# One product for the scales of all units, later weight squares, and the second batch's softmax sums in SBUF

## The chip, the cores and the metric

One core of a Trainium2 chip runs the whole program. The metric is the device time of one execution in microseconds (us). Three runs of the kernel before took 861.09, 863.54 and 863.58 us; their median is 863.54 us.

## The reference

Four batches of 576 tokens with 512 features pass through three stages.

1. Memory attention, per batch and head (8 heads of 64): `a = softmax(phi)` over 32 memory slots, `k_m = aᵀk`, `v_m = aᵀv`, then `softmax(q k_mᵀ / 8) v_m`.
2. A gated layer: `(sigmoid(x w_gate) * (x w_val)) w_out`, with 1536 hidden features.
3. A routed mixture of 8 experts: noisy logits, the two best experts of each token, `relu(x w1[e]) w2[e]` weighted by a softmax over the two.

The gated layer's weights arrive as 64-bit floats and are rounded to 32 bits on the chip. Products that need more than half precision are made of a high and a low 16-bit half of each operand.

## The kernel before

The program is written as Python generators that issue instructions for a planner. The planner lists each engine's instructions in a fixed order, chosen by priority and by data that it expects to be ready; on the chip each engine then runs its list strictly in order and waits at the head of it. `behind(d, o)` adds no wait of its own on the chip; it tells the planner that `d` stands after `o` in the order. `turns(g)` advances a generator by one `yield`, so the number of yields decides where in the program a step is issued. The attention generator runs with a priority 160 positions ahead once batch 0 is done.

**Rounding the weights** (`weights`, lines 371 to 414). There are 18 jobs: for each of six units of 256 hidden features a `wg` and a `wv` job (0 to 11), then six `wo` jobs (12 to 17). Every job has two halves of 512 KB. A half is loaded by SP's queue (line 352), and `rounded` (lines 359 to 369) makes 32-bit floats of it: ScalarE scales the low words (line 363), VectorE combines the high words (lines 367 and 368; `self.shifted` is the latest instruction of line 368), GpSimd adds the two (line 369). The loads of `wo` go into a ring of four buffers (`ws2`), so each waits for the GpSimd sum of the half that used its buffer four halves earlier.

**Scales.** When a job of the first twelve is rounded, ScalarE squares all of it into a sum (line 402). The sums of a unit go through a TensorE product with ones and three small VectorE instructions in `norm2` (lines 86 to 105), which give a power-of-two scale `s` and its inverse `iv` in tiles of that unit. `finish` (line 378) runs this two yields after the first rounding of the job after the unit. `unit_scales` (line 426) multiplies each unit's scale with each batch's scale `sv[b]`, two GpSimd instructions for every pair of batch and unit, as soon as both are known (lines 433 and 435).

**Fold and first stage.** `fold(b, u)` (line 243) scales the batch's memory values on GpSimd (line 250, needs `wss` from line 433), multiplies them into the unit's weights on TensorE (line 257) and splits the product on ScalarE and VectorE (lines 259 and 261). `stage1` (line 456) makes 24 matmuls for 192 tokens and one unit (line 468, `self.gated` is the latest of them), with tanh on ScalarE (470, `gss` from line 435), a product on VectorE (472), and the high and low half of the result on ScalarE and VectorE (473, 474). Eighteen such pieces belong to batch 0; after each of them the weights advance by three yields and, early on, the attention of batch 1 by one. The first six pieces of batch 1 follow.

**Attention of a batch** (`attention`, line 266). There are three pieces: two of 512 columns and one of 128. `scores` makes the products (lines 279 and 282) in a bank of the pool `pg`, whose four banks `stage1` and `fold` use too; VectorE takes the maximum and subtracts it (286, 290), ScalarE exponentiates (291). `normalised` sums on VectorE (line 297) into the same PSUM bank, adds 1e-9 (300) and inverts (301), and GpSimd multiplies (302). `turned` transposes on TensorE (310) and splits into `x` (317, 318). Batch 0 does its three sums after its three scores; the others do each sum right after its scores, in the same step.

**After that** come the `wo` scale and its splits (410 to 418), the second product (`stage2`, line 485), routing (`tokens`, `route`) and the experts (`first2` line 832, `second2` line 846).

Of the kernel before, what the change touches and what calls it, by code (L numbers as in the profile page):

```python
# [26 lines left out]
P = 128  # L27
# [11 lines left out]
A_BITS = 14  # L39
# [29 lines left out]
class Kern:  # L69
# [13 lines left out]

        self.tc.add_manual_dep(d.ins, o.ins.name, mybir.DependencyInfo(mybir.DependencyClass.NoSync, mybir.DependencyReason.DATA), reason="order")

    def norm2(self, pool, m, tag, before=1, n=1, floor=0):


        nc = self.nc
        for _ in range(before):  # L90
            yield
        pt = self.pr.tile([P, 512], F32, tag="pr", name="pmx")[:, :n]
        d = nc.tensor.matmul(pt, self.onef, m, start=True, stop=True)
        if self.mark is not None:
            self.behind(d, self.mark)

        s, iv = (pool.tile([P, n], I32, tag=tag + c, name=tag + c) for c in "si")
        h = pt.bitcast(I32)
        d = nc.vector.tensor_scalar(h, h, 24, 23, op0=ALU.logical_shift_right, op1=ALU.logical_shift_left)
        self.behind(d, self.less[1])  # L100
        if floor:
            nc.vector.tensor_scalar(h, h, floor << 23, None, op0=ALU.max)
        nc.vector.tensor_scalar(s, h, -1, 204 << 23, op0=ALU.mult, op1=ALU.add)
        nc.vector.tensor_scalar(iv, h, 50 << 23, None, op0=ALU.add)
        return s.bitcast(F32), iv.bitcast(F32)
# [160 lines left out]
    def attention(self, b):  # L266

        nc, a2, al = self.nc, self.a2, self.al
        kbd, x = self.kbd, self.xT[b]
        qt = [al[(b, "q", g)] for g in range(2)]  # L270
        def scores(u):

            nt = 1 if u == 2 else SC
            ps = self.pg.tile([P, SC, P], F32, tag="pg", name="pa")
            for pr in range(2):
                cols = slice(pr * 64, pr * 64 + 64)
                if u == 2:
# [12 lines left out]
            self.less.append(nc.vector.tensor_tensor(ex, sc, mx.unsqueeze(2).to_broadcast([P, n, M]), op=ALU.subtract))  # L290
            nc.scalar.activation(ex, ex, AF.Exp, scale=0.125)
            return ps, ex, n

        def normalised(ps, ex, n):
            sm = a2.tile([P, 4 * SC], F32, tag="ssm", name="ssm")[:, :n]
            tot = ps[:, 0, :n]
            d = nc.vector.tensor_reduce(tot, ex, axis=AX.X, op=ALU.add)
            if b == 0:
                self.behind(d, self.shifted)
            nc.vector.tensor_scalar(sm, tot, 1e-9, None, op0=ALU.add)  # L300
            nc.vector.reciprocal(sm, sm)
            nc.gpsimd.tensor_tensor(ex, ex, sm.unsqueeze(2).to_broadcast([P, n, M]), op=ALU.mult)
            return ex

        def turned(u, ex):
            nt = 1 if u == 2 else SC
            at = ex.rearrange("p (t h) m -> p t (h m)", t=nt)
            pt = self.bank(b)
            for t in range(nt):
                self.mark = nc.tensor.transpose(pt[:, t, :], at[:, t, :], self.idf)  # L310
            if u == 2:
                src = pt[:, 0, :].rearrange("p (g s) -> p g s", g=2)
                oh, ol = (x[:, l, :, SC * P :] for l in range(2))
            else:
                src = pt.rearrange("p a b -> p (a b)")
                oh, ol = (x[:, l, u, : SC * P] for l in range(2))
            nc.scalar.activation(oh, src, AF.Copy, scale=2.0 ** A_BITS)
            d = nc.vector.scalar_tensor_tensor(ol, src, 2.0 ** A_BITS, oh, op0=ALU.mult, op1=ALU.subtract)
            if b == 0:
                self.behind(d, self.shifted)  # L320
        part, ex = {}, {}
        for i in range(3):
            part[i] = scores(i)
            if b == 0 and i < 2:
                yield
                continue
            for j in range(3) if b == 0 else (i,):
                ex[j] = normalised(*part[j])
                yield
        if b:  # L330
            yield
        for i in range(3):
            turned(i, ex[i])
            yield
            self.tokens_ready = b * S + (SC * P if i == 1 else S if i == 2 else 0)
            if b + 1 < B:
                for y in ((("phi", 0), ("phi", 1), ("kv0", 0)), (("kv1", 0),), (("kv0", 1), ("kv1", 1)))[i]:
                    self.wanted.append((b + 1, *y))
# [32 lines left out]
    def weights(self):  # L371

        nc, cp = self.nc, self.cp
        self.wom = cp.tile([P, 6], F32, name="wom")
        junk = self.flat(self.wob[0][:, 0]).bitcast(BF16)
        sums = {}

        def finish(u, wait):

            s, iv = yield from self.norm2(cp, sums[u], f"w{u}", wait, 2)  # L380
            self.sw.append(s)
            self.iwg.append(iv[:, 0:1])
            self.iwv.append(iv[:, 1:2])
            self.unit_scales()
            yield

        for n, (kind, u) in enumerate(self.wjobs):
            v = self.flat(self.W[n]) if kind != "wo" else self.flat(self.wob[u + 1]).bitcast(F32)
            for h in range(2):
                self.rounded(self.wts[2 * n + h], v[:, h * 512 : (h + 1) * 512].bitcast(I32))  # L390
                self.wload_next()
                yield
                if h == 0 and 2 <= n <= 12 and n % 2 == 0:
                    yield from finish(n // 2 - 1, WAIT_W)
            if kind == "wo":
                for x in [u - 1] * (u > 0) + [u] * (u == UN - 1):
                    f = self.flat(self.wob[x + 1]).bitcast(F32)
                    self.behind(nc.scalar.activation(junk, f, AF.Square, scale=self.iwv[x], accum_out=self.wom[:, x : x + 1]), self.tanh)
            else:
                if kind == "wg":  # L400
                    sums[u] = cp.tile([P, 2], F32, tag="wum", bufs=2, name="wum")
                d = nc.scalar.activation(junk, v, AF.Square, accum_out=sums[u][:, n % 2 : n % 2 + 1])
                if self.tokens_ready:
                    self.behind(d, self.copied)
# [21 lines left out]
    def unit_scales(self):  # L426

        gp = self.nc.gpsimd
        for b in self.sv:
            for u in range(len(self.sw)):  # L430
                if (b, u) not in self.ws:
                    s = self.ws[(b, u)] = self.wss[:, b, u]
                    gp.tensor_scalar(s, self.sw[u], self.sv[b], 2.0 ** -A_BITS, op0=ALU.mult, op1=ALU.mult)
                    g = self.gs[(b, u)] = self.gss[:, b, u]
                    gp.tensor_scalar(g, self.iwg[u], self.invx[b], 0.5, op0=ALU.mult, op1=ALU.mult)

    def batch_scales2(self, b):
        t = self.cp.tile([P, 1], F32, name=f"it{b}")
# [791 lines left out]
```

## Time and profile before

| | |
|---|---|
| median of three runs | 863.54 us |
| profiled execution | 861.13 us |
| its span, first to last instruction | 859.4 us |
| mean granted TensorE clock | 0.967 |
| TensorE busy | 804.5 us, 94% |
| VectorE busy | 453.2 us, 53% |
| ScalarE busy | 441.0 us, 51% |
| GpSimd busy | 239.1 us, 28% |

The profiled execution's own time is 1.7 us above its span and 2.4 us below the median. Shares of busy time are means over stages that differ: what a change in one stage is worth is read from that stage's waits. PE is TensorE, PEld its weight loads, DVE VectorE, ACT ScalarE, POOL GpSimd, SP the queue that issues most transfers. A row's `<-` after an idle time names what ended the wait, inferred from semaphores. A clock of 1.00 is TensorE's 2.4 GHz, 0.50 is 1.2 GHz.

### The profile page before, as it was taken

The numbers are of one execution on the slowest core, as the hardware profiler recorded it, in microseconds if no ns is written. First come the engines' busy times: TensorE is split into PE (matmuls) and PEld (weight loads), VectorE is DVE, ScalarE is ACT, GpSimd is POOL, SyncE is SP. The second block draws the span as 40 slices with busy tenths as digits, with TensorE's granted clock in tenths as the row PEclk, the third lists the DMA queues.
The fourth block names the chain that finished last, engine by engine and source line by source line (L and its number), as shares of the span: only waits on it lengthen the run. The fifth ranks groups of instructions, "written<-read, shape, count | busy, mean of one in ns | idle before, by whom it ended". The sixth has DMA issues, their size and how long they took to land.

```text
span 859.4 us, 16748 instructions
## 1 busy us (share of the span) xinstructions
PE 804.5 (94%) x6531; PEld 528.6 (62%) x6531; DVE 453.2 (53%) x1221; ACT 441.0 (51%) x859; POOL 239.1 (28%) x285
## 2 busy tenths in 40 slices
PE   4698778999999998999999999999999999999995
PEld 3477655567667766777466555756657466574752
DVE  3787678445737697645474255743535444450210
ACT  4677568324545566644155456753646454461320
POOL 1755460021305021212116451113133231232012
PEclk8589889999999999999999999999999999999998
DMA  9977539631221675436966899625867758472113
GB/s 299 357 240 243 154 117 331 209 105 25 33 76 25 198 220 174 135 111 124 270 172 177 165 236 209 189 52 147 209 146 122 189 121 193 72 123 37 24 21 41
DMA packets 124609, 130.95 MB, mean 152 GB/s; under 512 B 71664, under 2 KB 88176, under 8 KB 124144
## 3 DMA queue, kind: packets, MB, share of 16 engines
q1 hardware_dynamic: 114480, 109.10, 44.7%
q0 software_dynamic: 10048, 20.76, 13.4%
q8 instruction: 52, 0.85, 0.4%
q14 instruction: 29, 0.24, 0.1%
HBM read 85.87 MB, written 28.76 MB: 133 GB/s over the span
## 4 chain that ended last, share of the span: by engine, by line
PE 72%; DMA 5%; DVE 4%; ACT 3%; issue 1%; POOL 0%; SPq 0%; POOLq 0%; DVEq 0%; ACTq 0%
PE py L846 23%; PE ph L832 21%; PE px L485 14%; PE pg L468 10%; DMA wsp<-hl 1%; PE pv L257 1%; DMA xt<-row 1%; PE pa L282 1%; DMA xg<-xs,mts 1%; DMA w<-wo 1%; DVE wo L418 1%; DVE wq L261 1%; PE pa L202 0%; DMA xe<-xg 0%; PE pl L513 0%
## 5 line engine op out<-in xcount | busy, mean ns | idle before, releaser
L468 PE MATMUL pg<-x,wq 128*128 128x192 f16 x1728 | 163.9, 251 | 12.9 <-ACT sg L470 4.7
L468 PEld LDWEIGHTS <-wq 128*128 128x128 f16 x1728 | 147.3, 100 | 31.1 <-issue 18.0
L846 PEld LDWEIGHTS <-hT 128*128 128x128 f16 (+1 forms) x960 | 99.9, 105 | 104.3 <-DVE hT L838 0.7
L485 PE MATMUL px<-wo,gT 128*128 128x512 f16 x648 | 148.4, 380 | 0.0
L854 POOL DMA_INDIRECT out<-y,mts x40 | 66.1, 1653 | 205.9 <-ACT y L853 203.8
L846 PE MATMUL py<-w2a,hT 128*128 128x512 f16 (+1 forms) x480 | 105.3, 379 | 0.2 <-DVE hT L838 0.2
L846 PE MATMUL py<-w2b,hT 128*128 128x512 f16 (+1 forms) x480 | 104.9, 379 | 0.0
L485 PEld LDWEIGHTS <-gT 128*128 128x128 f16 x648 | 62.1, 98 | 68.5 <-issue 3.3
L832 PE MATMUL ph<-xe,w1a 128*128 128x312 f16 (+2 forms) x768 | 103.3, 296 | 0.0
L832 PE MATMUL ph<-xe,w1b 128*128 128x312 f16 (+2 forms) x768 | 103.0, 296 | 0.0
L838 DVE TENSOR_TENSOR hT<-r,hT 128x312 f16<-128x312 f32 (+2 forms) x128 | 57.4, 480 | 83.9 <-ACT hT L837 83.6
L832 PEld LDWEIGHTS <-w1b 128*128 128x128 f16 x768 | 75.2, 98 | 27.1
L832 PEld LDWEIGHTS <-w1a 128*128 128x128 f16 x768 | 75.0, 98 | 27.2 <-issue 0.2
L853 ACT ACTIVATE y<-py,css 128x512 f32<-128x512 f32 (+1 forms) x40 | 27.4, 686 | 124.7 <-PE py L846 120.3
L836 ACT ACTIVATE r<-ph 128x312 f32<-128x312 f32 (+2 forms) x128 | 49.6, 428 | 73.7 <-PE ph L832 68.2
L639 POOL DMA_INDIRECT meta<-mt,vi x36 | 38.5, 1069 | 114.8 <-DVE vi L636 48.4
L817 POOL DMA_INDIRECT xg<-xs,mts x40 | 44.4, 1111 | 81.8 <-DMA xe<-xg 47.3
L470 ACT ACTIVATE sg<-pg,gss 128x384 f32<-128x384 f32 x72 | 41.9, 582 | 41.6 <-PE pg L468 41.2
L472 DVE SCALAR_TENSOR_TENSOR pg<-sg,pg 128x384 f32<-128x384 f32 x72 | 40.1, 557 | 37.2 <-PE pg L468 23.2
L473 ACT ACTIVATE gT<-pg 128x384 f16<-128x384 f32 x72 | 35.0, 487 | 37.6 <-DVE pg L472 37.4
L837 ACT CAST hT<-r 128x312 f16<-128x312 f32 (+2 forms) x128 | 53.1, 458 | 0.9
L851 DVE TENSOR_TENSOR css<-mts,iw 128x1 f32<-128x1 f32 (+1 forms) x40 | 6.4, 163 | 87.0 <-ACT y L853 80.3
(303 smaller groups left out, 957.6 us busy)
## 6 DMA issues: line engine op xcount, KB each, us to landing
wo<-w SPq DMA_DIRECT2D x52, 512.0 KB, 5.4
st<-kv SPq DMA_DIRECT2D x16, 512.0 KB, 6.9
w<-wo SPq DMA_DIRECT2D x12, 512.0 KB, 4.2
f<-w SPq DMA_DIRECT2D x12, 512.0 KB, 5.6
wsp<-hl SPq DMA_DIRECT2D x12, 512.0 KB, 3.6
out<-z SPq DMA_DIRECT2D x23, 256.0 KB, 3.1
xs<-row SPq DMA_DIRECT2D x18, 256.0 KB, 2.8
st<-q SPq DMA_DIRECT2D x6, 576.0 KB, 4.9
```

What stands on the lines that cost most here:

```text
L468: self.gated = nc.tensor.matmul(p[:, f, :], w[:, l, g, j, f * P : (f + 1) * P], x[:, r, g, ch * QC : (ch + 1) * QC], start=n == 0, stop=n ...
L470: self.tanh = nc.scalar.activation(sg, ps[0], AF.Tanh, scale=self.gs[(b, u)])
L472: nc.vector.scalar_tensor_tensor(pv, sg, 1.0, pv, op0=ALU.add, op1=ALU.mult)
L485: nc.tensor.matmul(p, g[:, l, f % 2, t * P : (t + 1) * P], self.wob[f // 2][:, r, f % 2, :], start=f + i == 0, stop=f == FT - 1 and i == 2)
L639: d = nc.gpsimd.indirect_dma_start(out=self.meta, out_offset=bass.IndirectOffsetOnAxis(ap=vi[:, t, k : k + 1], axis=0), in_=mt[:, t, k, :] ...
L817: self.nc.gpsimd.indirect_dma_start(out=xg.rearrange("p a b -> p (a b)"), out_offset=None, in_=self.xs[:rows, :], in_offset=bass.IndirectO ...
L832: self.first = nc.tensor.matmul(p[:, : t1 - t0], w1[:, l, k, f * P : (f + 1) * P], xe[:, x, t0:t1], start=n == 0, stop=n == 3 * KT - 1)
L836: nc.scalar.activation(r, p[:, : t1 - t0], AF.Relu, scale=2.0 ** -19)
L837: d = nc.scalar.copy(self.hT[:, 0, f, t0:t1], r)
L838: self.parted = d, nc.vector.tensor_sub(self.hT[:, 1, f, t0:t1], r, self.hT[:, 0, f, t0:t1])
L846: d = nc.tensor.matmul(py, self.hT[:, l, f, i * P : i * P + m], w2[:, w, f, :], start=n == 0, stop=n == 3 * F2T - 1)
L854: d = nc.gpsimd.indirect_dma_start(out=self.out, out_offset=bass.IndirectOffsetOnAxis(ap=mt[:m, 0:1], axis=0), in_=y[:m], in_offset=None, ...
```

## The change

It has three parts.

1. `unit_scales` issues one pair of GpSimd instructions for each batch and all of its units that are still missing, in place of one pair for each unit. For that the units' scales stand side by side in two tiles, `sws` and `swi`, that `norm2` writes into.
2. The squares of the jobs 3 to 11 are issued after the first half of the next job has been rounded, in place of right after the job's own second half. The jobs 0 to 2 stay as they are. `finish` keeps its place, two yields later.
3. In the batches 1 to 3 the softmax sum goes into the SBUF tile `ssm`, no longer into the PSUM bank of the scores. In batch 1 each sum is issued one step later: the first after the second scores, the second after the third, the third in a step that was empty. Its sums and the low halves of its `x` stand behind the latest rounding on VectorE (`self.shifted`), and its transposes behind the latest matmul of the first stage (`self.gated`).

```
--- before.py
+++ after.py
@@ -83,7 +83,7 @@
 
         self.tc.add_manual_dep(d.ins, o.ins.name, mybir.DependencyInfo(mybir.DependencyClass.NoSync, mybir.DependencyReason.DATA), reason="order")
 
-    def norm2(self, pool, m, tag, before=1, n=1, floor=0):
+    def norm2(self, pool, m, tag, before=1, n=1, floor=0, out=None):
 
 
         nc = self.nc
@@ -94,7 +94,7 @@
         if self.mark is not None:
             self.behind(d, self.mark)
 
-        s, iv = (pool.tile([P, n], I32, tag=tag + c, name=tag + c) for c in "si")
+        s, iv = out or (pool.tile([P, n], I32, tag=tag + c, name=tag + c) for c in "si")
         h = pt.bitcast(I32)
         d = nc.vector.tensor_scalar(h, h, 24, 23, op0=ALU.logical_shift_right, op1=ALU.logical_shift_left)
         self.behind(d, self.less[1])
@@ -293,9 +293,9 @@
 
         def normalised(ps, ex, n):
             sm = a2.tile([P, 4 * SC], F32, tag="ssm", name="ssm")[:, :n]
-            tot = ps[:, 0, :n]
+            tot = sm if b else ps[:, 0, :n]
             d = nc.vector.tensor_reduce(tot, ex, axis=AX.X, op=ALU.add)
-            if b == 0:
+            if b < 2:
                 self.behind(d, self.shifted)
             nc.vector.tensor_scalar(sm, tot, 1e-9, None, op0=ALU.add)
             nc.vector.reciprocal(sm, sm)
@@ -308,6 +308,8 @@
             pt = self.bank(b)
             for t in range(nt):
                 self.mark = nc.tensor.transpose(pt[:, t, :], at[:, t, :], self.idf)
+                if b == 1:
+                    self.behind(self.mark, self.gated)
             if u == 2:
                 src = pt[:, 0, :].rearrange("p (g s) -> p g s", g=2)
                 oh, ol = (x[:, l, :, SC * P :] for l in range(2))
@@ -316,7 +318,7 @@
                 oh, ol = (x[:, l, u, : SC * P] for l in range(2))
             nc.scalar.activation(oh, src, AF.Copy, scale=2.0 ** A_BITS)
             d = nc.vector.scalar_tensor_tensor(ol, src, 2.0 ** A_BITS, oh, op0=ALU.mult, op1=ALU.subtract)
-            if b == 0:
+            if b < 2:
                 self.behind(d, self.shifted)
         part, ex = {}, {}
         for i in range(3):
@@ -324,9 +326,14 @@
             if b == 0 and i < 2:
                 yield
                 continue
-            for j in range(3) if b == 0 else (i,):
+            for j in range(3) if b == 0 else (i - 1,) if b == 1 and i else (i,) if b > 1 else ():
                 ex[j] = normalised(*part[j])
+                if b == 0:
+                    yield
+            if b:
                 yield
+        if b == 1:
+            ex[2] = normalised(*part[2])
         if b:
             yield
         for i in range(3):
@@ -372,17 +379,26 @@
 
         nc, cp = self.nc, self.cp
         self.wom = cp.tile([P, 6], F32, name="wom")
+        self.sws, self.swi = (cp.tile([P, 6, 2], I32, name=n) for n in ("sws", "swi"))
         junk = self.flat(self.wob[0][:, 0]).bitcast(BF16)
         sums = {}
 
         def finish(u, wait):
 
-            s, iv = yield from self.norm2(cp, sums[u], f"w{u}", wait, 2)
+            s, iv = yield from self.norm2(cp, sums[u], f"w{u}", wait, 2, out=(self.sws[:, u], self.swi[:, u]))
             self.sw.append(s)
             self.iwg.append(iv[:, 0:1])
             self.iwv.append(iv[:, 1:2])
             self.unit_scales()
             yield
+
+        def square(n):
+            u = n // 2
+            if n % 2 == 0:
+                sums[u] = cp.tile([P, 2], F32, tag="wum", bufs=2, name="wum")
+            d = nc.scalar.activation(junk, self.flat(self.W[n]), AF.Square, accum_out=sums[u][:, n % 2 : n % 2 + 1])
+            if self.tokens_ready:
+                self.behind(d, self.copied)
 
         for n, (kind, u) in enumerate(self.wjobs):
             v = self.flat(self.W[n]) if kind != "wo" else self.flat(self.wob[u + 1]).bitcast(F32)
@@ -390,18 +406,16 @@
                 self.rounded(self.wts[2 * n + h], v[:, h * 512 : (h + 1) * 512].bitcast(I32))
                 self.wload_next()
                 yield
+                if h == 0 and 4 <= n <= 12:
+                    square(n - 1)
                 if h == 0 and 2 <= n <= 12 and n % 2 == 0:
                     yield from finish(n // 2 - 1, WAIT_W)
             if kind == "wo":
                 for x in [u - 1] * (u > 0) + [u] * (u == UN - 1):
                     f = self.flat(self.wob[x + 1]).bitcast(F32)
                     self.behind(nc.scalar.activation(junk, f, AF.Square, scale=self.iwv[x], accum_out=self.wom[:, x : x + 1]), self.tanh)
-            else:
-                if kind == "wg":
-                    sums[u] = cp.tile([P, 2], F32, tag="wum", bufs=2, name="wum")
-                d = nc.scalar.activation(junk, v, AF.Square, accum_out=sums[u][:, n % 2 : n % 2 + 1])
-                if self.tokens_ready:
-                    self.behind(d, self.copied)
+            elif n < 3:
+                square(n)
             yield
         m = cp.tile([P, 1], F32, name="wom1")
         nc.vector.tensor_reduce(m, self.wom, axis=AX.X, op=ALU.add)
@@ -427,12 +441,13 @@
 
         gp = self.nc.gpsimd
         for b in self.sv:
-            for u in range(len(self.sw)):
-                if (b, u) not in self.ws:
-                    s = self.ws[(b, u)] = self.wss[:, b, u]
-                    gp.tensor_scalar(s, self.sw[u], self.sv[b], 2.0 ** -A_BITS, op0=ALU.mult, op1=ALU.mult)
-                    g = self.gs[(b, u)] = self.gss[:, b, u]
-                    gp.tensor_scalar(g, self.iwg[u], self.invx[b], 0.5, op0=ALU.mult, op1=ALU.mult)
+            us = [u for u in range(len(self.sw)) if (b, u) not in self.ws]
+            if us:
+                r = slice(us[0], us[-1] + 1)
+                gp.tensor_scalar(self.wss[:, b, r], self.sws.bitcast(F32)[:, r], self.sv[b], 2.0 ** -A_BITS, op0=ALU.mult, op1=ALU.mult)
+                gp.tensor_scalar(self.gss[:, b, r, 0], self.swi.bitcast(F32)[:, r, 0], self.invx[b], 0.5, op0=ALU.mult, op1=ALU.mult)
+                for u in us:
+                    self.ws[(b, u)], self.gs[(b, u)] = self.wss[:, b, u], self.gss[:, b, u]
 
     def batch_scales2(self, b):
         t = self.cp.tile([P, 1], F32, name=f"it{b}")
```

## Rows read from the trace of the kernel before

**Rows 1.** The page, part 1 (busy time) and part 2 (granted clock, 40 slices).

```profile
PE 804.5 (94%) x6531; PEld 528.6 (62%) x6531; DVE 453.2 (53%) x1221; ACT 441.0 (51%) x859; POOL 239.1 (28%) x285
...
PEclk8589889999999999999999999999999999999998
```

**Rows 2.** Busy time by stretch: PE, PEld, DVE, ACT, POOL (instructions), clock, DMA, GB/s.

```profile
40.00:80.00 40.00, 35.57 (x440) 28.43 (x438) 35.58 (x78) 31.73 (x72) 22.72 (x33) 0.90 0.76 238
80.00:125.00 45.00, 32.59 (x341) 26.79 (x341) 31.70 (x66) 27.05 (x53) 24.31 (x28) 0.85 0.51 160
...
160.00:296.00 136.00, 135.17 (x1350) 93.34 (x1349) 77.15 (x263) 60.21 (x120) 28.39 (x56) 1.00 0.31 83
300.00:800.00 500.00, 495.06 (x3470) 309.94 (x3469) 249.40 (x661) 257.99 (x481) 135.37 (x115) 1.00 0.65 155
```

**Rows 3.** The chain of waits from 105 us: start, us, what.

```profile
110.24 0.03 POOL ex L302
110.26 5.78 DMA w<-wo
...
125.60 3.56 DMA wrf<-rn
```

**Rows 4.** Who TensorE waited for, 76 to 125 us: total, times, longest.

```profile
PE pg L468 <- DVE ssm L300: 3.6, 2, 2.2
PE pa L310 <- POOL ex L302: 3.2, 2, 1.8
PE pa L282 <- ACT sg L470: 2.5, 1, 2.5
PE pg L468 <- ACT sg L470: 2.3, 1, 2.3
```

**Rows 5.** The timeline, 72 to 100 us: start, us, engine, line, tile, [idle before].

```profile
76.64 0.27 POOL L433 TENSOR_SCALAR wss<-w0s,sv1s 128x2 f32<-128x2 f32 x1 [2.71 <-DVE sv1i L104]
...
79.11 1.92 PE L282 MATMUL pa<-kbd,st 128*128 128x64 f32 x16
...
80.55 0.27 POOL L435 TENSOR_SCALAR gss<-w4i,sv0i 128x1 f32<-128x1 f32 x1
...
80.78 2.53 POOL L369 TENSOR_TENSOR w<-w,w 128x512 int32<-128x512 int32 x2
...
83.34 1.06 ACT L402 ACTIVATE wo<-w 128x1024 bf16<-128x1024 f32 x1 [2.94 <-POOL w L369]
...
85.49 0.55 ACT L470 ACTIVATE sg<-pg,gss 128x384 f32<-128x384 f32 x1
...
86.10 3.68 PE L282 MATMUL pa<-kbd,st 128*128 128x64 f32 x16 [2.50 <-ACT sg L470]
...
95.31 1.18 POOL L250 TENSOR_TENSOR vs<-vb,wss 128x256 f32<-128x256 f32 x2
```

**Rows 6.** Busy time by fine stretch, columns as in rows 2.

```profile
86.00:88.00 2.00, 1.90 (x9) 1.91 (x10) 1.55 (x3) 0.94 (x3) 0.65 (x2) 0.50 0.44 164
...
92.00:93.00 1.00, 0.96 (x19) 0.37 (x4) 0.00 (x0) 0.39 (x1) 0.58 (x1) 0.66 0.26 86
...
120.00:124.30 4.30, 1.98 (x42) 1.32 (x27) 4.00 (x7) 3.40 (x8) 3.55 (x4) 1.00 0.01 3
```

**Rows 7.** The timeline, 100 to 135 us, columns as in rows 5.

```profile
103.34 2.19 PE L257 MATMUL pv<-w,vs 64*32 64x256 f32 x32
...
106.68 0.29 DVE L297 TENSOR_REDUCE pa<-ex 128x4 f32<-128x128 f32 x1 [0.88 <-ACT ex L291]
...
107.69 2.55 POOL L369 TENSOR_TENSOR wo<-wo,w 128x512 int32<-128x512 int32 x2 [1.30 <-DVE ssm L300]
...
116.06 0.67 ACT L363 ACTIVATE w<-w 128x512 int32<-128x512 uint32 x1 [2.55 <-DMA w<-wo]
...
124.31 1.15 PE L468 MATMUL pg<-x,wq 128*128 128x192 f16 x12 [2.33 <-ACT sg L470]
```

**Rows 8.** Line 582's instructions: ns min/median/max, starts, forms.

```profile
L582 DVE TENSOR_SCALAR az<-lg x9: 163/175/176, 189.8 to 444.7; 128x16 f32<-128x16 f32 x9
```

More of the change, by code (lines that the diff above doesn't have):

```diff
@@ L84, in behind, with norm2 @@
         self.tc.add_manual_dep(d.ins, o.ins.name, mybir.DependencyInfo(mybir.DependencyClass.NoSync, mybir.DependencyReason.DATA), reason="order")
-    def norm2(self, pool, m, tag, before=1, n=1, floor=0):
+    def norm2(self, pool, m, tag, before=1, n=1, floor=0, out=None):
         nc = self.nc
@@ L95, in norm2 @@
             self.behind(d, self.mark)
-        s, iv = (pool.tile([P, n], I32, tag=tag + c, name=tag + c) for c in "si")
+        s, iv = out or (pool.tile([P, n], I32, tag=tag + c, name=tag + c) for c in "si")
         h = pt.bitcast(I32)
@@ L295, in normalised @@
             sm = a2.tile([P, 4 * SC], F32, tag="ssm", name="ssm")[:, :n]
-            tot = ps[:, 0, :n]
+            tot = sm if b else ps[:, 0, :n]
             d = nc.vector.tensor_reduce(tot, ex, axis=AX.X, op=ALU.add)
-            if b == 0:
+            if b < 2:
                 self.behind(d, self.shifted)
@@ L310, in turned @@
                 self.mark = nc.tensor.transpose(pt[:, t, :], at[:, t, :], self.idf)
+                if b == 1:
+                    self.behind(self.mark, self.gated)
             if u == 2:
@@ L318, in turned @@
             d = nc.vector.scalar_tensor_tensor(ol, src, 2.0 ** A_BITS, oh, op0=ALU.mult, op1=ALU.subtract)
-            if b == 0:
+            if b < 2:
                 self.behind(d, self.shifted)
@@ L326, in attention @@
                 continue
-            for j in range(3) if b == 0 else (i,):
+            for j in range(3) if b == 0 else (i - 1,) if b == 1 and i else (i,) if b > 1 else ():
                 ex[j] = normalised(*part[j])
+                if b == 0:
+                    yield
+            if b:
                 yield
+        if b == 1:
+            ex[2] = normalised(*part[2])
         if b:
@@ L374, in weights @@
         self.wom = cp.tile([P, 6], F32, name="wom")
+        self.sws, self.swi = (cp.tile([P, 6, 2], I32, name=n) for n in ("sws", "swi"))
         junk = self.flat(self.wob[0][:, 0]).bitcast(BF16)
@@ L378, in finish @@
         def finish(u, wait):
-            s, iv = yield from self.norm2(cp, sums[u], f"w{u}", wait, 2)
+            s, iv = yield from self.norm2(cp, sums[u], f"w{u}", wait, 2, out=(self.sws[:, u], self.swi[:, u]))
             self.sw.append(s)
@@ L385, in finish, with square @@
             yield
+        def square(n):
+            u = n // 2
+            if n % 2 == 0:
+                sums[u] = cp.tile([P, 2], F32, tag="wum", bufs=2, name="wum")
+            d = nc.scalar.activation(junk, self.flat(self.W[n]), AF.Square, accum_out=sums[u][:, n % 2 : n % 2 + 1])
+            if self.tokens_ready:
+                self.behind(d, self.copied)
         for n, (kind, u) in enumerate(self.wjobs):
@@ L392, in weights @@
                 yield
+                if h == 0 and 4 <= n <= 12:
+                    square(n - 1)
                 if h == 0 and 2 <= n <= 12 and n % 2 == 0:
@@ L398, in weights @@
                     self.behind(nc.scalar.activation(junk, f, AF.Square, scale=self.iwv[x], accum_out=self.wom[:, x : x + 1]), self.tanh)
[L399 to L404, printed above, removed]
+            elif n < 3:
+                square(n)
             yield
@@ L429, in unit_scales @@
         for b in self.sv:
[L430 to L435, printed above, removed]
+            us = [u for u in range(len(self.sw)) if (b, u) not in self.ws]
+            if us:
+                r = slice(us[0], us[-1] + 1)
+                gp.tensor_scalar(self.wss[:, b, r], self.sws.bitcast(F32)[:, r], self.sv[b], 2.0 ** -A_BITS, op0=ALU.mult, op1=ALU.mult)
+                gp.tensor_scalar(self.gss[:, b, r, 0], self.swi.bitcast(F32)[:, r, 0], self.invx[b], 0.5, op0=ALU.mult, op1=ALU.mult)
+                for u in us:
+                    self.ws[(b, u)], self.gs[(b, u)] = self.wss[:, b, u], self.gss[:, b, u]
     def batch_scales2(self, b):
```

## The prediction

> **What bounds the kernel now.** I began with the page: TensorE is busy 94% of the span [rows 1], so the first question is where the other 6% lies. The stretches answer it. From 160 to 296 us TensorE is busy 135.2 of 136 us, and from 300 to 800 us 495 of 500 [rows 2]. There a faster GpSimd, ScalarE or VectorE buys nothing, and what comes earlier before 160 us should make the end earlier by as much. The 12 us from 80 to 125 in which TensorE does nothing are another matter [rows 2], and the change works there. No engine is full in that stretch: VectorE has 31.7 of 45 us, while from 40 to 80 us it had 35.6 of 40, or 89% [rows 2]. So it is waits, not work, that make the stretch long.
>
> Third I read who TensorE waited for from 76 to 125 us: the add of line 300 (3.6 us), the GpSimd product of line 302 (3.2), and tanh on ScalarE twice (2.5 and 2.3) [rows 4]. Fourth, the timeline, to see why. At 76.64 us GpSimd begins a run of ten products for unit scales, with one fold between them, that lasts until the roundings start at 80.78 [rows 5]. The roundings end at 83.31. The weight square on ScalarE has waited 2.94 us for them; the tanh behind it starts only at 85.49, and TensorE stands 2.50 us until 86.10 [rows 5]. Then the granted clock falls: it is 0.50 (1.2 GHz) from 86, and the 0.66 of the slice 92 to 93 puts its return to 1.00 (2.4 GHz) at about 92.7 [rows 6]. The page's strip of clocks shows this fall in the fifth slice (86 to 107 us) and a second one in the sixth [rows 1]. In that stretch the sixteen score products of line 282 take 3.68 us; those at 79.11, at full clock, took 1.92 [rows 5]. Last, the chain of waits: what the listing shows of it starts at 110.24 us with the load of a `wo` half, issued when GpSimd has finished the roundings of 107.69 to 110.24 [rows 3, 7], and it goes on to the load of 125.60 [rows 3], which needs all `wo` roundings done. So the end moves if the `wo` roundings move.
>
> **The change, part by part.** The sum is made against the profiled execution, 861.1 us, which is 2.4 us below the median of 863.5; I carry the gain over to the median.
>
> (1) *Scales.* Of the ten products from 76.64 us, batch 1 needs two for units 0 to 3, or for 0 to 4 if unit 4 is known by then; the other pair of unit 4 stays: four to six remain. At 0.27 us each, or 4.1 us for the ten with a fold between [rows 5], four to six products are 1.1 to 2.2 us less. A product over five units has ten elements per partition instead of two, and no row has that size. I take the same 0.27 us, with nothing as the lower bound of the extra and the 0.59 us of a fold (half of a 1.18 us pair, 256 elements [rows 5]) as the upper. Batches 2 and 3 save ten products each, which lie beside a full TensorE [rows 2]: nothing.
>
> (2) *Squares.* Nine of them, of 1.06 us [rows 5], move behind the next job's first rounding. Their work is the same; what goes is ScalarE's wait for GpSimd, 2.94 us at the worst place [rows 5]. Queued behind that wait were two roundings and the tanh that TensorE needed. With (1) and (2) TensorE's 2.50 us go. The price is that a unit's scale comes later by one rounding, some 1.3 us. It is covered: for unit 5 the scaled values are done at 96.5 and TensorE folds at 103.34 [rows 5, 7]. If that cover were gone, the 1.3 us would stand before a fold.
>
> (3) *The clock.* Without the 2.50 us idle there is no fall at 86. The fall costs at least the 1.76 us of those scores (3.68 less 1.92) [rows 5] and at most half of its 6.7 us [rows 6], 3.35. I take 2.7, about the middle, because TensorE was busy all through 86 to 92 [rows 6] but with short products too. Together (1) to (3) give 2.5 + 2.7 = 5.2 us.
>
> (4) *Sums in SBUF.* The bank is free once line 290 has subtracted, so the two waits for line 300 (3.6 us [rows 4]) go. The sum and the add change one operand's place. The nearest row, an add of the same 128x16 shape from SBUF to SBUF, takes 175 ns [rows 8]; I take no difference, with one such add more or less per piece as bounds, 0.5 us either way for batch 1.
>
> (5) *Order.* Transposes behind the latest first-stage matmul: TensorE does those matmuls instead of waiting for line 302 (3.2 us [rows 4]). Sums behind roundings: at 106.68 us VectorE stood 0.88 us for an exponential, with the `wo` rounding of the chain behind it, and GpSimd 1.30 us for that [rows 7]; this turns round. Behind a sum there now wait the product of line 302 and the transposes. One piece is later by a step, and the cover is the rest of batch 0's first stage, which still has matmuls at 124.31 [rows 7].
>
> (4) and (5) take away up to 6.8 us of TensorE's waits, but not so much of the time: VectorE has to fit. Its 31.7 us at the 89% of the stretch before need 35.6 us, so the 45 us can shrink by 9.4 at most. After (1) to (3) have taken 5.2 there is room for 4.2. I take 1.3 of it, a third: behind these waits stand others (the loads of `wo`, ScalarE's order) that the change doesn't touch.
>
> Sum: 5.2 + 1.3 = 6.5 us. 861.1 - 6.5 = 854.6 for the profiled execution; 863.5 - 6.5 = **857.0 us** on the median. Late next should be the tanh at 124.31 us, for which TensorE waits 2.33 us today [rows 7].
>
> **The rivals.** *Absorbed.* The waits of 80 to 110 us go, but `wo` sets the pace: each load takes 5.78 us, only four are under way, and ScalarE already waits 2.55 us for the one that lands at 116 [rows 3, 7]. For it: the listed chain starts with just this load. Against it: the load is issued behind roundings that were late through the very waits that go. It would leave about 1 us: 862.5.
>
> *Slower: a longer wait and a new fall of the clock between 112 and 125 us.* If TensorE arrives 5.2 us earlier at the first-stage piece of 124.31 while the roundings there keep their time, its idle time of 2.33 us there grows to 7.5. At 2.33 us the clock stayed at 1.00 [rows 6, 7]; after the 2.50 at 86 it fell [rows 5, 6]. A fall would come on top of a gain that is already eaten up: half of 6.7 us, some 3 us, 866.5. It decides if the `wo` loads come earlier by less than the matmuls. For it speaks ScalarE's wait for a load at 116.06 [rows 7], against it the same as above.
>
> *Port.* Line 300 stays a small VectorE add, but now both its sides are in SBUF. If it had to wait for a running GpSimd instruction, each of batch 1's three adds could lose a rounding's 1.27 us (2.53 for two [rows 5]): 3.8 us, 860.8. Against it, nine adds of this shape between SBUF tiles took 163 to 176 ns [rows 8], though no row shows GpSimd busy beside them. The Trainium skill (SBUF — State Buffer, Who interferes with whom) speaks for this rival: a VectorE `tensor_scalar` between SBUF operands may run in a mode that shares a port pair with GpSimd, and the later of the two blocks. By that rule the time would lie between 857.0 and 860.8; the nine adds neither confirm nor refute it.
>
> *Not what it says.* The planner orders anew, and the square may still stand ahead of an unfinished rounding; then only (1) is left, 1.1 to 2.2 us, about 862. I count this with "absorbed".
>
> **How the numbers follow.** Forecast 0.58, absorbed 0.17, slower 0.17, port 0.08. About 0.3% (2.6 us) is what a measurement of this kernel can tell from no change: below 861.0 is faster, above 866.1 slower. The forecast is faster, absorbed is the same, and the port is counted half as either: faster 0.62, same 0.21, slower 0.17. The forecast's own range: 5.2 of gain may be as little as 2.8 if (3) is at its lower end and (1) leaves part of the wait, and as much as 9.4 and the second fall's 3 us if VectorE is the only bound left, so 851 to 861. The range that should hold 8 in 10 adds "absorbed" and half of "slower": 851 to 866.5.
>
> **What would show each step.** In the profile after: fewer than half of the 48 products of lines 433 and 435; no square waiting for GpSimd for more than 1 us near the end of the `wv` jobs; no idle TensorE and no clock below 1.00 around 82 to 92 us; no wait of TensorE for the add after the sum; the chain's `wo` load issued 5 us earlier or more; from 160 us on the same picture, shifted. I am wrong if the clock falls as often as before in 80 to 125 us, if TensorE's wait for tanh at the last pieces of batch 0 has grown by as much as the others shrank, or if the full stretch starts at the same time as before.

## The result: 855.2 us, 0.9913 of the kernel before

The changed kernel takes 855.24 us (median of 6 runs, 852.53 to 856.79), the kernel before 862.55 (6 runs). The ratio is 0.9913, with a 95% interval of 0.9892 to 0.9934: 7.5 us faster. The profiled execution took 852.53 us, its span is 850.7. In the changed kernel line 359 is the load of a weight half (352 before), 376 the GpSimd rounding (369), 399 the weight square (402), 447 and 448 the unit scales (433, 435), 483 the first-stage matmul (468), 485 the tanh (470) and 489 the low half of `gT` (474).

Page of the changed kernel, parts 1 and 2, as [rows 1]:

```profile
PE 796.5 (94%) x6531; PEld 521.7 (61%) x6531; DVE 454.2 (53%) x1221; ACT 440.6 (52%) x859; POOL 232.3 (27%) x257
...
PEclk9599999999999999999999999999999999999998
```

GpSimd has 257 instructions instead of 285: of 48 products 20 are left. In the slices that hold 86 to 128 us the clock's strip now shows 9 where it showed 8, but one short fall is hidden in it, behind an idle TensorE at 94 to 96 us; before there were two falls, from 86 us and at 110 to 116. The stretches of the changed kernel, columns as in [rows 2]:

```profile
80.00:125.00 45.00, 36.20 (x466) 27.62 (x466) 40.48 (x90) 34.96 (x69) 25.66 (x47) 0.96 0.69 213
...
94.00:96.00 2.00, 0.00 (x0) 0.00 (x0) 2.00 (x7) 1.79 (x4) 1.84 (x2) 0.94 0.46 186
96.00:98.00 2.00, 1.62 (x11) 1.50 (x11) 1.32 (x4) 2.00 (x5) 1.60 (x3) 0.50 0.71 229
...
160.00:296.00 136.00, 133.72 (x1399) 94.19 (x1397) 81.46 (x278) 67.76 (x128) 23.30 (x38) 1.00 0.32 88
...
300.00:800.00 500.00, 492.37 (x3410) 308.90 (x3405) 242.21 (x639) 252.71 (x476) 133.05 (x112) 1.00 0.63 149
```

VectorE, 31.70 us of the 45 before, now has 40.48, which is 90%; the granted clock of the stretch is 0.96 instead of 0.85. Whom TensorE waits for from 76 to 125 us, as [rows 4]:

```profile
PE pg L483 <- ACT sg L485: 3.6, 2, 3.0
PE pv L257 <- ACT sg L485: 1.5, 2, 1.2
PE pg L483 <- DVE wq L261: 1.4, 2, 1.2
PE pmx L93 <- DVE wom L421: 1.1, 1, 1.1
```

The add of line 300 and the product of line 302, 3.6 and 3.2 us in [rows 4], are gone from the list. Tanh is left. The timeline of the changed kernel, as [rows 5]:

```profile
72.08 0.30 POOL L447 TENSOR_SCALAR wss<-sws,sv1s 128x10 f32<-128x10 f32 x1
...
73.05 0.28 POOL L448 TENSOR_SCALAR gss<-swi,sv1i 128x5 f32<-128x5 f32 x1
...
76.65 1.06 ACT L399 ACTIVATE wo<-w 128x1024 bf16<-128x1024 f32 x1
...
79.29 2.00 PE L282 MATMUL pa<-kbd,st 128*128 128x64 f32 x16
...
90.32 1.29 POOL L376 TENSOR_TENSOR wo<-wo,w 128x512 int32<-128x512 int32 x1 [1.03 <-ACT sg L485]
...
91.09 0.55 DVE L300 TENSOR_SCALAR ssm<-ssm 128x16 f32<-128x16 f32 x1
...
94.21 0.67 ACT L370 ACTIVATE w<-w 128x512 int32<-128x512 uint32 x1 [0.64 <-DMA w<-wo]
...
96.38 2.08 PE L483 MATMUL pg<-x,wq 128*128 128x192 f16 x12 [2.96 <-ACT sg L485]
...
109.89 1.15 PE L483 MATMUL pg<-x,wq 128*128 128x192 f16 x12 [0.67 <-ACT sg L485]
```

Batch 1's five first units get both scales in two products of 0.30 and 0.28 us. The square at 76.65 waits for nothing. The second sixteen scores, 3.68 us behind a 2.50 us gap in [rows 5], take 2.00 with no gap before them. The row of 109.89 is batch 0's last first-stage piece, which stood at 124.31 us before.

**A trap in these two profiles.** They suggest more than the change did. Against [rows 2] TensorE has 1.4 us less work from 160 to 296 us and 2.7 us less from 300 to 800, as if the gain were partly given back. On the other side the first product of stage one starts 3.6 us earlier (39.25 instead of 42.83), although no edit comes before it. Both are answered by running the kernel before once more (e5 below).

### The profile page after: what moved, and what is told of

It is laid out like the page before. It is cut to its first block, busy times and chain, and to the rows that moved or that the text cites. A ratio compares the mean times of both kernels' runs of the same rounds, so it can differ in the third digit from the quotient of the medians.

```text
span 850.7 us, 16713 instructions
## 1 busy us (share of the span) xinstructions
PE 796.5 (94%) x6531; PEld 521.7 (61%) x6531; DVE 454.2 (53%) x1221; ACT 440.6 (52%) x859; POOL 232.3 (27%) x257
## 4 chain that ended last, share of the span: by engine, by line
PE 76%; DVE 8%; DMA 6%; ACT 6%; issue 2%; POOL 1%; SPq 0%; another core or an unknown queue 0%; DVEq 0%; ACTq 0%; POOLq 0%
PE py L861 23%; PE ph L847 22%; PE px L500 14%; PE pg L483 11%; DMA st<-kv 2%; PE pv L257 2%; PE pa L282 1%; DMA wo<-wg 1%; DVE pw L374 1%; PE pa L202 1%; DMA f<-w 1%; DMA xt<-row 1%; DVE pg L487 1%; DVE gT L489 1%; DVE wq L261 1%
## 5 line engine op out<-in xcount | busy, mean ns | idle before, releaser
L483 PEld LDWEIGHTS <-wq 128*128 128x128 f16 x1728 | 144.7, 99 | 33.9 <-issue 16.5
L654 POOL DMA_INDIRECT meta<-mt,vi x36 | 38.5, 1070 | 117.5 <-DVE vi L651 47.8
```

Source lines behind the costliest of these rows:

```text
L483: self.gated = nc.tensor.matmul(p[:, f, :], w[:, l, g, j, f * P : (f + 1) * P], x[:, r, g, ch * QC : (ch + 1) * QC], start=n == 0, stop=n ...
L654: d = nc.gpsimd.indirect_dma_start(out=self.meta, out_offset=bass.IndirectOffsetOnAxis(ap=vi[:, t, k : k + 1], axis=0), in_=mt[:, t, k, :] ...
```

## The experiments

The experiments ran on four chips, and each ratio is to the kernel before on the same chip: e1 to e4 on one (kernel before 856.3 us), e5 to e8 on a second (863.1), e9 to e11 on a third (862.7), e12 on a fourth (855.7). Theories: **A**, the steps of the prediction; **B**, another part carries the gain; **C**, the gain is given back behind 160 us; the others are named where they come in. The table collects what follows; VectorE and clock are those of the stretch 80 to 125 us in the run's profile.

| run | what it has of the change | ratio (95%) | VectorE us | clock |
|---|---|---|---|---|
| e5 | nothing | 1 | 31.3 | 0.85 |
| e1 | scales | 0.9968 (0.9951 to 0.9984) | 34.1 | 0.89 |
| e2 | squares | 0.9980 (0.9964 to 0.9996) | 34.2 | 0.89 |
| e3 | scales, squares | 0.9953 (0.9936 to 0.9970) | 35.6 | 0.85 |
| e4 | sums in SBUF, order | 0.9944 (0.9924 to 0.9964) | 35.9 | 0.89 |
| e8 | scales, squares, sums in SBUF | 0.9975 (0.9952 to 0.9998) | 33.3 | 0.85 |
| e7 | scales, squares, order | 0.9902 (0.9868 to 0.9936) | 39.3 | 0.96 |
| e9 | all but the gated transposes | 0.9931 (0.9903 to 0.9959) | 38.5 | 0.92 |
| e10 | all but the tie behind roundings | 0.9931 (0.9905 to 0.9956) | 37.6 | 0.96 |
| e11 | all but the later step | 0.9927 (0.9901 to 0.9952) | 36.7 | 0.96 |
| e6 | all | 0.9911 (0.9883 to 0.9940) | 39.3 | 0.96 |
| e12 | all, tanh ahead of a rounding | 0.9892 (0.9854 to 0.9929) | 39.6 | 0.96 |

**e1, the scales alone.** The kernel before with the new `unit_scales` and its two tiles.

```diff
+                gp.tensor_scalar(self.wss[:, b, r], self.sws.bitcast(F32)[:, r], ...
+                gp.tensor_scalar(self.gss[:, b, r, 0], self.swi.bitcast(F32)[:, r, 0], ...
```

> The kernel before with the first part of the change alone: one product over all new units instead of one for each. Theory A (the prediction's steps): ten products near 76 us become four to six, ScalarE's wait of 2.94 us for the roundings shrinks by 1.1 to 2.2 us; TensorE's 2.50 us gap near 84 us is then 0.3 to 1.4 us, and whether the clock still falls behind it decides between 1 and 5 us of gain: 861 at the clock's fall, 857.5 without it; I take 860. Theory B (the two waits are one; the squares' place matters and not the products): within 1 us of the kernel before, 862. Theory C (what is won before 160 us is given back behind it, up to some 5 us): 862 to 862.5, though the first product of the last output stage begins earlier.

853.30 us against 856.34: 0.9968, or 2.7 us (1.4 to 4.2). Theory A's 860 stood against 862.5, a gain of 2.5. B (at most 1 us) and C (half a microsecond or less) fall.

**e2, the squares alone.**

```diff
+                if h == 0 and 4 <= n <= 12:
+                    square(n - 1)
```

> The kernel before with the second part alone: nine weight squares issued behind the first rounding of the next job. Theory A: ScalarE waits for no unfinished rounding, so its 2.94 us wait and most of TensorE's 2.50 us gap near 84 us go, and with them the clock's fall at 86 us: 5.2 less the 1.1 of the products that stay, some 4 us, 858.5. Theory B (the ten products keep the roundings late, and the tanh needs what is behind them): the gap only moves, under 1 us, 862. Theory C (given back behind 160 us): 861 to 862.5, with the clock's fall at 86 us gone all the same.

854.51 us, 0.9980, or 1.7 us (0.3 to 3.1). That is less than theory A's 4 us; B's "under 1 us" and C's lie within the interval. The products that stay hold the roundings up, as B said, but some of the gain is there: the gap before the second sixteen scores is 1.3 us instead of 2.50.

**e3, both.**

> The first two parts together, without the sums' new place and the new order. Theory A: 5.2 us of the 7.3 measured for the whole, 857.3, with no clock below 1.00 between 82 and 92 us and the waits of TensorE for the add and for the product of line 302 of the kernel before still there between 90 and 112 us. Theory B (the sums and the order carry most): under 3 us, 860 or more. Theory C (the stretch behind 160 us gives back whatever goes beyond some 5 us): the full gain here, 857, and again nearly the same for the third part alone, so the two sums come to more than the whole.

851.51 us, 0.9953: 4.0 us (2.6 to 5.5). e1 and e2 add to 4.4. Theory A's 5.2 lies within the interval, B's "under 3" at its lower end. Its account of the clock is another matter. Fine stretches of e3, columns as in [rows 2]:

```profile
86.00:88.00 2.00, 1.65 (x16) 1.07 (x17) 1.84 (x4) 1.29 (x3) 1.67 (x6) 1.00 0.58 176
98.00:100.00 2.00, 0.00 (x0) 0.00 (x0) 1.18 (x3) 2.00 (x5) 0.00 (x0) 1.00 0.63 139
104.00:106.00 2.00, 1.64 (x11) 1.36 (x9) 1.32 (x3) 0.96 (x3) 1.67 (x3) 0.50 0.25 100
```

The fall at 86 us is gone, as predicted, and it is gone in e1 and e2 too (1.00 from 80 to 98 us in both). TensorE now idles at 98 to 100 us instead and the clock falls behind that, and once more from 118 us: over the stretch from 80 to 125 us it is 0.85, as before. So these two parts won waiting time, and moved the clock's fall without taking it away. TensorE's waits for lines 300 and 302 are still there, 2.5 and 1.4 us; its two longest from 74 to 128 us (476 is the first-stage matmul, 478 the tanh):

```profile
PE pg L476 <- ACT sg L478: 2.7, 2, 2.1
PE pv L257 <- DVE ssm L300: 2.5, 1, 2.5
```

**e4, the third part alone.**

> The third part alone: the second batch's softmax sums in SBUF, its transposes behind the gated first-stage products, its sums and low halves behind roundings, one piece a step later. The products and squares stay as in the kernel before. Theory A: 1.3 us, 861.2, with the clock's fall at 86 us as before and no wait of TensorE for the add or the product of line 302. Theory B (this part carries most): 4 us or more, 858.5 or less. Theory C: 4 to 5 us, 858, and e3 and e4 together more than the whole's 7.3.

852.10 us, 0.9944: 4.8 us (3.1 to 6.5), more than the 1.3 us that the prediction gave it. Theory A is wrong here in size, though its signs are there (the clock still falls near 87 us, and TensorE waits for neither line 300 nor 302); B and C both fit. e3 and e4 together would be 0.9897, which the whole decides.

**e5, the kernel before again**, unchanged.

> The kernel before, unchanged, profiled on the same chip as the others. All theories: some 856 us, as the other runs of it on this chip. Theory A (the prediction's steps): the clock falls at 86 us again behind a gap of TensorE of some 2.5 us, and the first product of stage one starts within 1 us of the 42 us of e1, e3 and e4. Theory L (the start is luck): stage one starts anywhere from 39 to 43 us whatever the kernel, so up to 3.6 us of the 8.7 us between the two profiled spans belong to no edit; the slices before 40 us then look like those of one of the other runs.

862.99 us, span 861.2, stage one starts at 41.76. The run came out on another chip than e1 to e4, so the 856 us do not apply. Theory L holds for the start: 42.83 and 41.76 in two runs of this kernel, 39.67 in e2, 38.51 in e11, 39.25 and 42.14 in two runs of the whole. Its stretches:

```profile
80.00:125.00 45.00, 32.95 (x349) 25.66 (x347) 31.33 (x66) 27.88 (x54) 24.64 (x37) 0.85 0.46 150
...
160.00:296.00 136.00, 133.87 (x1339) 91.98 (x1337) 77.07 (x265) 59.24 (x116) 28.46 (x56) 1.00 0.30 79
...
300.00:800.00 500.00, 491.63 (x3452) 307.36 (x3450) 248.93 (x660) 257.07 (x479) 132.58 (x114) 1.00 0.63 155
```

On this chip the kernel before, too, has TensorE busy 133.87 and 491.63 us, not the 135.17 and 495.06 of [rows 2]. So the "given back" time needs no edit. That it goes with the chip is likely: in these two stretches e1 to e4, all on the first chip, have 135.05 to 135.18 and 494.56 to 495.81 us, e5 to e8, all on the second, 133.73 to 133.90 and 491.47 to 492.33. Its waits from 74 to 128 us, for the comparison with e6:

```profile
PE pa L310 <- POOL ex L302: 3.2, 2, 1.8
PE pg L468 <- DVE ssm L300: 2.6, 2, 2.2
PE pa L282 <- ACT sg L470: 2.5, 1, 2.5
PE pg L468 <- ACT sg L470: 2.2, 1, 2.2
```

**e6, the whole, on the same chip.**

> The whole change on the chip of e1 to e4. Theory A (additive): the ratios of e3 and e4 taken together, 0.9953 and 0.9944, give 0.990, or 847.6 us at 856.3 for the kernel before. Theory C (what goes beyond some 5 us is given back behind 160 us): no better than e4 alone, 0.9944 or 851.5 us, with more waits of TensorE between 200 and 440 us than in e3 or e4.

856.19 us against 863.10, on the chip of e5: 0.9911, as in the first measurement. A's 0.9897 lies inside the interval; C's 0.9944 lies just above its end at 0.9940. Stretches of e6:

```profile
80.00:125.00 45.00, 36.29 (x453) 28.81 (x450) 39.34 (x88) 34.75 (x69) 25.63 (x47) 0.96 0.66 205
...
160.00:296.00 136.00, 133.73 (x1389) 93.75 (x1387) 79.36 (x273) 64.61 (x123) 22.48 (x35) 1.00 0.31 80
...
300.00:800.00 500.00, 491.47 (x3419) 307.83 (x3420) 244.17 (x642) 252.57 (x476) 132.34 (x112) 1.00 0.63 151
```

Against e5 the two long stretches agree within 0.2 us: theory C falls here. The spans differ by 7.1 us (861.2 less 854.1), and the whole of that comes from the stretch before 160. It can be read from the first product of `stage2`, of e5 first:

```profile
L485 PE MATMUL px<-wo,gT x648: 376/379/390, 131.5 to 434.7; 128*128 128x512 f16 x162
```

```profile
L500 PE MATMUL px<-wo,gT x648: 376/379/390, 123.0 to 427.0; 128*128 128x512 f16 x162
```

It starts 8.5 us earlier, the last one 7.7, and 7.1 us are left at the end. Whom TensorE waited for in e6 from 74 to 128 us:

```profile
PE pg L483 <- ACT sg L485: 4.0, 2, 3.3
PE pv L257 <- ACT sg L485: 1.7, 2, 1.4
PE pg L483 <- DVE wq L261: 1.3, 2, 1.1
```

5.8 us of waits for lines 300 and 302 are gone, and the waits for tanh, 4.7 us in the two e5 rows, are 5.7. The queue of `wo` loads, in the two timelines, e5 first:

```profile
103.16 10.83 SPq L352 DMA_DIRECT2D w<-wo  x5
```

```profile
94.93 10.06 SPq L359 DMA_DIRECT2D w<-wo  x5
```

The last five `wo` loads are issued 8.2 us earlier; the prediction asked for 5 or more.

**e7, the sums back in PSUM, the rest kept.**

```diff
-            tot = sm if b else ps[:, 0, :n]
+            tot = ps[:, 0, :n]
```

> The whole change, with the sums of the later batches back in the PSUM bank and the new order kept. Theory A (the sums' place takes away TensorE's waits for the add of line 300, of up to 3.6 us): slower than the whole by 1 to 3 us and a wait for that add shows again, 850 us. Theory B (behind the roundings the sum comes late anyway, and nobody needs the bank so soon): the same within 1 us, and no wait for the add. Theory P (a VectorE add between SBUF tiles is held up by GpSimd; 0.55 and 0.28 us in the changed kernel's trace): faster by 0.5 us.

854.75 us, 0.9902: no slower than the whole. TensorE's waits in e7 from 74 to 128 us:

```profile
PE pg L483 <- DVE ssm L300: 0.8, 1, 0.8
PE pv L257 <- DVE ssm L300: 0.6, 1, 0.6
```

The wait for the add does come back, 1.4 us, and costs nothing that can be seen. Of theory A's 1 to 3 us nothing shows, though its lower end can't be excluded: against e6 the interval reaches 0.0025, or 2.2 us. P's 0.5 us can't be told from B's nothing either.

**e8, the old order, the sums kept in SBUF.** The whole without the two ties `if b < 2` (again `if b == 0`), the tie of the transposes and the later step.

```diff
-                if b == 1:
-                    self.behind(self.mark, self.gated)
...
-            for j in range(3) if b == 0 else (i - 1,) if b == 1 and i else (i,) if b > 1 else ():
+            for j in range(3) if b == 0 else (i,):
```

> The whole change, with the second batch's old order: sums not tied behind roundings, transposes not behind the gated products, no piece a step later; the sums stay in SBUF. Theory A (the order takes away TensorE's waits for the product of line 302): slower than the whole by 1 to 3 us, 850 us, with 1 to 3 us of such waits. Theory B (the order only moves the waits to the tanh): the same within 1 us. Theory C (the order is what gives back behind 160 us): faster than the whole by 1 us or more.

861.48 us, 0.9975. The order is worth 0.0064 of 863 us, 5.5 us, more than theory A said; the two intervals do not meet. TensorE's waits in e8, same window (476 is its first-stage matmul, 478 the tanh, 482 the low half of `gT`):

```profile
PE pg L476 <- ACT sg L478: 6.4, 3, 3.1
PE pa L310 <- POOL ex L302: 2.6, 2, 1.5
PE pg L476 <- DVE gT L482: 1.5, 1, 1.5
```

e3 differs from e8 in the place of the sums alone. Of e3's two rows the wait for line 300, 2.5 us, is gone here, and the one for tanh has grown from 2.7 to 6.4. Freeing the bank alone moved the wait to another producer, and e8's ratio is no better than e3's 0.9953. Against e3, on another chip, e7 gives the order alone 0.0051, or 4.4 us.

**e9, e10 and e11, one element of the order taken away each.**

> The whole change, but the second batch's transposes are not put behind the latest first-stage product. The whole measured 0.9911 and without all of the order 0.9975: 5.5 us to be shared out. Theory A (TensorE's order: it stood 2.6 us for the product of line 302 where the old order was kept): 0.994 or more, 858 us at 863 for the kernel before, with 1 us or more of that wait. Theory B (VectorE's and GpSimd's order is what counts: sums behind roundings, a step later): 0.991 to 0.992, since the product then comes early enough anyhow.

> The whole change, but the second batch's sums and low halves are not tied behind the roundings. Theory B (a sum that waits for its exponential holds the rounding behind it, and with it the chain through the wo loads): 0.993 or more, 857 us at 863, and VectorE waits for an exponential 0.5 us or more with a rounding behind it. Theory A: 0.991 to 0.992. Theory S (the step's delay alone does it, the tie only follows): also 0.991 to 0.992, and e11 takes it all.

> The whole change, but each piece's sum stands in the same step as its scores, not a step later. Theory S: 0.994 or more, 858 us at 863, with TensorE waiting for the product of line 302 or VectorE for the exponential. Theory A or B: 0.991 to 0.992, with the transposes and sums kept back by their ties all the same.

856.75, 857.16 and 856.14 us against 862.67. Each is 0.0016 to 0.0020 above the whole, 1.4 to 1.7 us, inside the intervals, and the whole itself was not run on this chip. A, B and S are not told apart: e10 just reaches the 0.993 that B asked, e9 and e11 miss the 0.994 of A and S. The three together are worth 5.5 us (e8), so it is likely, not shown, that each gives a share. Of the signs that were named, e9 has the wait of TensorE for line 302's product (1.5 us), as A asked; in e10 VectorE waits for no exponential, against B; e11 shows neither wait that S named. Stretches from 80 to 125 us, of e9, e10 and e11 in turn:

```profile
80.00:125.00 45.00, 35.51 (x425) 27.08 (x423) 38.53 (x84) 32.44 (x66) 24.35 (x47) 0.92 0.62 190
```

```profile
80.00:125.00 45.00, 33.48 (x432) 25.41 (x439) 37.62 (x84) 32.31 (x63) 23.54 (x46) 0.96 0.60 184
```

```profile
80.00:125.00 45.00, 32.90 (x421) 24.98 (x424) 36.65 (x85) 32.79 (x64) 24.20 (x46) 0.96 0.59 187
```

VectorE has 38.53, 37.62 and 36.65 us there, between e8's 33.3 and the whole's 39.3.

**e12, the tanh ahead of a `wo` rounding's low half**, the whole with

```diff
         if self.tokens_ready:
             self.behind(d, self.copied)
+        if late:
+            self.behind(d, self.tanh)
```

where `late` holds for the `wo` halves.

> The whole change, and the low half of a wo rounding stands behind the latest tanh on ScalarE. In the whole, what is late next is the tanh at 99.4 us: ScalarE stands 1.00 us for a wo load that lands at 97.86, with two casts and the tanh queued behind it, and TensorE waits 3.31 us, with the clock at 0.50 behind that. Theory A (what is late next is this order on ScalarE): that wait shrinks below 1 us and the dip of the clock near 101 us goes: 2 to 4 us, ratio 0.987. Theory W (the wo loads set the pace from there on, so the end moves only with them): within 1 us of the whole, 0.991, and TensorE waits for the tanh or the cast elsewhere before 125 us.

847.82 us against 855.65: 0.9892 (0.9854 to 0.9929). It can't be told from the whole. Its timeline shows where that tanh stands (485 is its first-stage matmul, 487 the tanh):

```profile
93.46 0.69 ACT L370 ACTIVATE w<-w 128x512 int32<-128x512 uint32 x1 [0.95 <-DMA w<-wo]
...
94.98 0.59 ACT L487 ACTIVATE sg<-pg,gss 128x384 f32<-128x384 f32 x1
...
95.62 1.15 PE L485 MATMUL pg<-x,wq 128*128 128x192 f16 x12 [2.58 <-ACT sg L487]
```

The low half still stands ahead of that tanh, waits 0.95 us for its load, and TensorE waits 2.58. The edit put other low halves behind a tanh (two of the four that follow each other from 85.20 us in the profile of after stand at 88.60 and 89.55 here), not this one, so the question of theory A against W isn't answered. The fall of the clock near 101 us that A named is gone, but one shows at 108 to 112 us. No version was shown to beat the changed kernel; e7 and e12 are level with it.

## Why the prediction was right, step by step

**The time and the range.** 6.5 us were predicted, 7.5 and 7.7 measured (0.9913, 0.9911), and 855.24 lies in the range. That the sum came out near is in part luck: (4) and (5) alone gave 4.8 us where 1.3 were summed (e4), and (1) to (3) alone 4.0 where 5.2 were (e3, whose interval still holds 5.2).

**(1) Scales: right in kind.** 48 products became 20, and e1 alone is 2.7 us faster. The run that begins at 76.64 us has twelve products, not the ten that the prediction counted. Four of them are left, and with the fold among them they take 1.80 us instead of 4.14: 2.3 us less, where 1.1 to 2.2 were forecast. A product over ten elements took 0.30 us, over two 0.27, so the size costs next to nothing, as was taken.

**(2) Squares: right in kind.** No square waits for GpSimd near the end of the `wv` jobs and the gap of 2.50 us is gone. e3's 4.0 us (2.6 to 5.5) for (1) to (3) hold the 2.5 us of the gap.

**(3) The clock: right about the fall at 86 us, not shown as a gain.** The fall at 86 us went, but e3 has a fall at 102 us instead and the same 0.85 over the stretch. Of its 4.0 us 1.5 remain beside the gap's 2.5 where the step summed 2.7; the interval allows both. With the order alone the clock is 0.89 (e4). It reaches 0.96 only where the first two parts and the order, or most of it, meet (e6, e7, e10, e11, e12). Why it does there is open: from 90 to 110 us TensorE is idle no less in e6 (busy 15.03 of 20 us) than in e3 (15.30). The step looked at the one gap that the change closes, not at the next one.

**(4) Sums in SBUF: wrong as a gain.** The waits for line 300 went, and were worth nothing that the runs can tell: without the order the wait turns up at the tanh (e8), with it the old place is as good (e7).

**(5) Order: right in kind, too small by a factor of nearly four.** Of the 4.2 us of room under VectorE's ceiling the prediction took a third, 1.3, for (4) and (5) together, because other waits stand behind. e4 measures the two at 4.8 us (3.1 to 6.5), and the order alone is worth 4.4 (e7 against e3) to 5.5 (e6 against e8). The ceiling itself held about: it was set at 89% of a stretch, and VectorE stands at 39.34 of 45 us in e6, 87%, and at 90% in the profile of after. The mis-sized term is the "third": such a wait is there (the tanh below), but it took far less than two thirds of the room. In the table the ratio falls as VectorE's time in the stretch rises, nearly in step; ScalarE's rises as well (27.88 us in e5, 34.75 in e6), so it is not shown that VectorE sets the limit.

**From 160 us on the same picture, shifted: right.** e5 and e6 agree there within 0.2 us in both stretches, and the first product of `stage2` starts 8.5 us earlier.

**Late next, the tanh at 124.31: wrong.** That piece stands at 109.89 us in the profile of after, and its wait has shrunk from 2.33 to 0.67 us. Late is the tanh before 96.38. On ScalarE a low half that waits for its `wo` load stands ahead of it, as the row of 94.21 shows. That is a piece of the "absorbed" rival: the loads came 8.2 us earlier, and one of them still holds ScalarE up for 0.64 us there (0.95 in e12). How much of TensorE's 3 us hangs on it was not shown.

**The rivals.** Absorbed fell with the ratio; its 5.78 us are one load, while the median of the twelve `wo` loads was 4.2. Slower fell too: the wait that should have grown to 7.5 us is the 0.67 at 109.89, and from 100 to 125 us the granted clock is 1.00 in the profile of after. "Not what it says" fell with the first rows: the square at 76.65 waits for nothing. **Port**: the wait it named exists. The add at 91.09 us took 0.55 us where nine adds of [rows 8] took 163 to 176 ns; it ended at 91.64, just behind the GpSimd rounding that ran from 90.32 to 91.61. The Trainium skill (SBUF — State Buffer, Who interferes with whom) says that the later of such two instructions blocks, and this row agrees. But of the three adds of batch 1 only this one met it so; the price is 0.4 us, not 1.27 each (the third, a smaller one, took 0.28 us). e6 and e12 have an add of 0.54 and 0.55 us at the same place, and in e8 no add took more than 175 ns.

## What to carry to other kernels

When a stretch is long through waits, read how full the next engine is in it: here the room up to that engine's best share elsewhere, 9.4 us, was nearer to the 7.5 measured than the sum of TensorE's four waits, 11.6 us. A wait taken away on its own can return at another producer, as in e8. What paid here was a new order of the engines' lists, not a bank set free; which part of the order pays was not told apart. Before two profiles are compared stretch by stretch, profile the old kernel again on the same chip: a difference far behind the edit need not come from the edit.

## What was not expected of the hardware

The same kernel takes 856.3 us on one chip and 863.1 on another, and the difference seems to have a place. From the first product of `stage2` to the end the four kernels on the first take 722.4 to 724.6 us (e1 to e4), the four on the second 729.7 to 732.2 (e5 to e8), whatever their order. The two chips have only different kernels to compare, and the first profile of the kernel before, whose chip is not on record, lies between: 725.7 us, with the long stretches of the first chip in [rows 2]. What stands behind it was not looked into.

The start of stage one, ahead of every edit, varied by 4.3 us between runs (38.51 to 42.83), and a granted clock of 0.50 (1.2 GHz) followed idle time of TensorE in the three places looked at: 2.50 us in [rows 5], the empty 94 to 96 us in the profile of after, the empty 98 to 100 us in e3. Not every idle piece had a fall behind it: the 2.33 us before 124.31 in [rows 7] had none.
